# Second Fourier axis folded once more: five short matmuls in place of four long ones, joined on VectorE

**Chip, cores, metric.** One core of a Trainium2 chip. The metric is the device time of one execution in microseconds (us), median over several executions. In the lines of the profile PE is TensorE (the matmuls), DVE VectorE and ACT ScalarE (elementwise work), POOL GpSimd, and SPq the queue in which SyncE issues DMAs (copies); PSUM is the memory that the matmuls write.

## The reference, cut to what matters

Attention reads between `x` (8 batches, 512 rows, 8 heads of 64) and a small `state` (32 rows) give 544 rows of 512 for each batch. On these rows:

```python
X = np.fft.fft(x, axis=1)                 # first axis: the 544 rows
X = np.fft.fft(X, axis=2)                 # second axis: 512 columns
u = x + np.real(X)
un = (u - u.mean(-1)) / sqrt(u.var(-1) + 1e-6)
out = u + np.maximum(un @ w_ch1, 0.0) @ w_ch2     # 512 -> 2048 -> 512
```

## The kernel before: the parts concerned

Columns are folded once (d with 512-d), rows are folded too. `over_s` transforms along the rows, `over_d` along the columns (this is the "second axis"), `add` adds the input to it, `centre` takes statistics and writes the centred tile `ub` in bf16, and `turn_u` transposes it into `unT`, which the first MLP layer (`layer1`, PSUM tile `ph`) reads. `layer2` (PSUM tile `po`) ends in a store through `ot`.

```python
def fold():                                            # VectorE, once a batch
    nc.vector.tensor_add(Sm, XF, XR)
    nc.vector.tensor_add(XE[:, 0:2, :], Sm[:, :, 0:256], Sm[:, :, 512:256:-1])
    ...                                                # XO = difference, XN = middle column
def over_d(k):                                         # TensorE, twice a batch
    yp = yp_of[k] = qt("yp")
    for c in range(4):
        nc.tensor.matmul(yp, lhsT=G[:, c, 128 * k:128 * k + 128], rhs=T2[:, c, :],
                         start=(c == 0), stop=(c == 3))
def add(k, r):                                         # VectorE, PSUM + SBUF
    if r:
        nc.vector.tensor_add(U[k][:, 1, 1:512], yp[:, 1:512], XR[:, k, 1:512])
        nc.vector.tensor_add(U[k][:, 1, 512:513], yp[:, 0:1], XR[:, k, 512:513])
    else:
        nc.vector.tensor_add(U[k][:, 0, 0:512], yp, XF[:, k, 0:512])
...
for b in range(1, B + 1):       # a stage: layer 2 of batch b-1, layer 1 of b, reads and transform of b+1
    streams = [(layer2(b - 1) + ..., 0, 1)]
    streams.append((layer1(b), 0.08 if b == 1 else 0.02, 1))
    streams.append((reads_next, 0, 0.4))               # where in the stage a stream begins and ends
    streams.append((transform(b + 1), 0.45, 0.92))
    ...
    weave(*streams)             # sorts the steps of all streams: the order of issue
```

The softmax here doesn't subtract the row's maximum and nothing guards it: scores larger than these inputs give would overflow.

## Time and profile before

| | before |
|---|---|
| time, median of 3 runs | 329.02 us (328.88 to 329.29) |
| TensorE / VectorE / ScalarE busy | 96% / 51% / 44% |
| time of the profiled execution (its span) | 331.23 us (329.3 us) |
| first matmul of the second layer (`po`) begins | 61.8 us |
| from there to the end of the span | 267.5 us |

The table splits the span in two. Up to the first `po` the engines wait for each other; from it to the end TensorE has no visible gap, so a microsecond of TensorE work is a microsecond of time there. The lines themselves are in the prediction.

### The profile page before, as it was taken

Reading aid. Unit: us, or ns where it says so; the run is one execution under the profiler, and the core shown is the slowest. Engines: PE = TensorE matmul, PEld = TensorE weight load, DVE = VectorE, ACT = ScalarE, POOL = GpSimd, SP = SyncE. Lnnn points to the kernel's source line nnn. Section 1 sums busy time; section 2 is a strip of 40 time slices with the busy share of each in tenths; the row PEclk is TensorE's granted clock in tenths of the full one; section 3 lists DMA queues with packets and bytes.
Section 4 is the critical chain, followed back from the end, with each engine's and each line's share of the span. In section 5 each row is a group of like instructions: output and inputs, shape, how many; then the busy total and the mean of one; then the engine's idle time right before and its main releaser. Section 6 shows DMA issues by size and latency. Waiting matters only on the chain.

```text
span 329.3 us, 5692 instructions
## 1 busy us (share of the span) xinstructions
PE 315.1 (96%) x2204; PEld 182.2 (55%) x2204; DVE 169.0 (51%) x421; ACT 146.3 (44%) x279; POOL 62.8 (19%) x144
## 2 busy tenths in 40 slices
PE   6988969899999999999999999999999999999995
PEld 6776858645555554556555554545554544455444
DVE  8778575553755556671554728363855375100112
ACT  7897827844344344334344244434344423233300
POOL 3189732400240012200240003200210021000000
PEclk9999979999999999999999999999999999999999
DMA  7999999174155905259152433630241215222055
GB/s 150 171 145 216 159 196 187 32 157 100 48 104 120 180 2 113 50 130 169 50 112 66 97 66 79 128 82 32 64 98 36 60 50 112 58 57 64 34 118 137
DMA packets 107082, 33.15 MB, mean 101 GB/s; under 512 B 98480, under 2 KB 102832, under 8 KB 107056
## 3 DMA queue, kind: packets, MB, share of 16 engines
q1 hardware_dynamic: 96336, 27.03, 38.0%
q0 software_dynamic: 4224, 4.19, 8.0%
q10 hardware_dynamic: 6496, 1.57, 2.3%
q8 instruction: 17, 0.28, 0.4%
q14 instruction: 9, 0.07, 0.1%
HBM read 22.04 MB, written 13.63 MB: 108 GB/s over the span
## 4 chain that ended last, share of the span: by engine, by line
PE 84%; DVE 5%; DMA 4%; POOL 3%; SPq 2%; ACT 1%; issue 1%; DVEq 0%; POOLq 0%; ACTq 0%
PE po L646 35%; PE ph L580 32%; PE yp L473 3%; DMA xs<-in_x_dram 3%; PE gp L455 3%; PE ph L590 2%; PE eTp L331 2%; PE srp L378 2%; SPq L108 1%; PE xrp L359 1%; POOL w L269 1%; DMA out_dram<-ot 1%; PE xfp L359 1%; PE gp L459 1%; PE esp L342 1%
## 5 line engine op out<-in xcount | busy, mean ns | idle before, releaser
L646 PE MATMUL po<-w,hT 128*128 128x512 bf16 x496 | 125.2, 379 | 0.0
L582 ACT ACTIVATE hT<-ph 128x512 bf16<-128x512 f32 x112 | 66.8, 597 | 111.1 <-PE ph L580 111.0
L580 PE MATMUL ph<-unT,w 128*128 128x512 bf16 x448 | 115.0, 379 | 0.0
L580 PEld LDWEIGHTS <-w 128*128 128x128 bf16 x576 | 51.1, 98 | 50.0
L646 PEld LDWEIGHTS <-hT 128*128 128x128 bf16 x496 | 48.0, 98 | 45.5
L611 DVE SCALAR_TENSOR_TENSOR ot<-po,rstd,U 128x512 f32<-128x512 f32 (+1 forms) x33 | 24.2, 734 | 47.7 <-PE po L646 45.3
L465 POOL COPY GL<-G 128x128 bf16<-128x128 bf16 x8 | 2.4, 301 | 135.9 <-ACT G L463 135.9
L479 DVE TENSOR_TENSOR U<-yp,XR 128x511 f32<-128x511 f32 x16 | 10.9, 684 | 29.3 <-PE yp L473 29.3
L279 DVE BATCH_NORM_STATS2 st<-U 128x6 f32<-128x512 f32 x32 | 21.8, 682 | 0.1
L284 POOL TENSOR_TENSOR rstd<-rstd,mhalf 128x1 f32<-128x1 f32 x34 | 20.0, 588 | 2.7
L283 POOL TENSOR_TENSOR rstd<-mv,epst 128x1 f32<-128x1 f32 x34 | 7.2, 211 | 63.6 <-DVE mv L281 63.5
L590 PE MATMUL ph<-unT,w 128*128 128x128 bf16 x256 | 18.0, 228 | 0.0
L666 PE MATMUL warm<-ident 128*128 128x128 bf16 x172 | 14.2, 237 | 3.6 <-POOL ident masks.py:199 3.3
L463 ACT CAST G<-gp 128x288 bf16<-128x288 f32 x30 | 11.8, 398 | 12.0 <-PE gp L455 8.9
L590 PEld LDWEIGHTS <-w 128*128 128x128 bf16 x256 | 16.6, 103 | 0.5
L473 PE MATMUL yp<-T,G 128*128 128x512 bf16 x64 | 16.4, 379 | 0.0
L666 PEld LDWEIGHTS <-ident 128*128 128x128 bf16 x172 | 12.5, 108 | 4.9 <-POOL ident masks.py:199 3.3
L389 ACT ACTIVATE XR<-srp,rcs 32x64 bf16<-32x64 f32 x32 | 9.9, 309 | 10.3 <-DVE rcs L380 10.0
L359 PEld LDWEIGHTS <-ET 128*128 128x128 bf16 x80 | 7.3, 98 | 11.7 <-DVE XF L368 3.7
L117 POOL CAST xin<-xs 128x2048 bf16<-128x2048 f32 x7 | 13.2, 1890 | 0.0
L592 ACT ACTIVATE hT<-ph 128x512 bf16<-128x512 f32 x16 | 9.4, 604 | 8.0 <-PE ph L590 8.0
L492 DVE TENSOR_SCALAR ub<-U,mv 128x512 bf16<-128x512 f32 x24 | 12.3, 512 | 0.9
(137 smaller groups left out, 339.4 us busy)
## 6 DMA issues: line engine op xcount, KB each, us to landing
xs<-in_x_dram SPq DMA_DIRECT2D x30, 256.0 KB, 5.0
w<-in_moe_w_ch_dram POOLq DMA_DIRECT2D x8, 512.0 KB, 9.9
out_dram<-ot SPq DMA_DIRECT2D x15, 256.0 KB, 2.2
r_dram<-ot SPq DMA_DIRECT2D x14, 256.0 KB, 4.4
out_dram<-r_dram SPq DMA_DIRECT2D x14, 256.0 KB, 3.5
xs<-in_x_dram ACTq DMA_DIRECT2D x2, 256.0 KB
l_dram<-ot SPq DMA_DIRECT2D x2, 256.0 KB, 2.0
r_dram<-ot ACTq DMA_DIRECT2D x2, 256.0 KB
```

The costliest lines, as they stand in the source:

```text
L117: nc.gpsimd.tensor_copy(t[:, :, 1:513], xs)
L279: nc.vector.bn_stats(st6, u)
L284: nc.gpsimd.tensor_tensor(rstd, rstd, mhalf, op=ALU.pow)
L359: nc.tensor.matmul(ph[:, 0:260], lhsT=ET[:, g, c0:c0 + 128], rhs=rhs, start=True, stop=True)
L473: nc.tensor.matmul(yp, lhsT=G[:, c, 128 * k:128 * k + 128], rhs=T2[:, c, :], start=(c == 0), stop=(c == 3))
L492: nc.vector.tensor_scalar(t, in0=ud, scalar1=mv[:, 0:1], scalar2=None, op0=ALU.subtract)
L580: nc.tensor.matmul(ph[:, o:o + n], lhsT=w1[:, c, f * 128:(f + 1) * 128], rhs=un_of[key][:, c, :], start=(c == 0), stop=(c == DC - 1))
L582: nc.scalar.activation(hT[:, per * i:per * i + per, :].rearrange("p a b -> p (a b)"), ph, AF.Relu, scale=-1.0 if key in flipped else 1.0)
L590: nc.tensor.matmul(ph[:, o:o + 128], lhsT=w1[:, c, f * 128:(f + 1) * 128], rhs=un_of[key][:, c, 128 * r:128 * r + 128], start=(c == 0), st ...
L611: nc.vector.scalar_tensor_tensor(ot[:, cols], in0=po_of[i][:, 0:cols.stop - cols.start], scalar=rstd, in1=u[:, cols], op0=ALU.mult, op1=AL ...
L646: nc.tensor.matmul(po_of[i], lhsT=h_of[key][:, f, i * 128:(i + 1) * 128], rhs=w2[:, f, :], start=(f == 0), stop=(f == FC - 1))
L666: nc.tensor.matmul(t[:, 0:128], lhsT=ident, rhs=ident, start=(i == 0), stop=(i == n - 1))
```

## The change

The intent is less TensorE work. Even outputs of the second axis need only a cosine over d folded with 256-d, odd outputs the difference; so five matmuls of about 128 columns give all values, even ones in the first half of the PSUM bank and odd ones in the second. The price: the fold has a second step on VectorE (`XQ`), ScalarE copies the odd half to SBUF, and VectorE joins even and odd into `y` before the two additions. The order of issue is changed with it.

```diff
 def fold():
-    nc.vector.tensor_add(XE[:, 0:2, :], Sm[:, :, 0:256], Sm[:, :, 512:256:-1])
+    nc.vector.tensor_add(XE[:, 0:2, 0:256], Sm[:, :, 0:256], Sm[:, :, 512:256:-1])   # XE, XO now fp32
...
+    nc.vector.tensor_add(XQ[:, 0], XE[:, :, 0:128], XE[:, :, 256:128:-1])
+    nc.vector.tensor_sub(XQ[:, 1], XE[:, :, 0:128], XE[:, :, 256:128:-1])
...
+    nc.vector.tensor_sub(XQ[:, 2], XO[:, :, 0:128], XO[:, :, 256:128:-1])
+    nc.vector.tensor_add(XQ[:, 3], XO[:, :, 128:0:-1], XO[:, :, 128:256])
+def parts(g):
+    p = qt("yp")
+    nc.tensor.matmul(p[:, 0:129], lhsT=g[0], rhs=TE[:, 0:129], start=True, stop=False)
+    nc.tensor.matmul(p[:, 0:129], lhsT=g[2], rhs=TN, start=False, stop=True)
+    nc.tensor.matmul(p[:, 257:384], lhsT=g[2], rhs=TO[:, 0:127], start=True, stop=True)
+    nc.tensor.matmul(p[:, 129:257], lhsT=g[1], rhs=TE[:, 129:257], start=True, stop=True)
+    nc.tensor.matmul(p[:, 384:512], lhsT=g[3], rhs=TO[:, 127:255], start=True, stop=True)
+    odd = wk.tile([128, 256], F32, name="odd", tag="odd", bufs=1)
+    nc.scalar.copy(odd, p[:, 256:512])
+def whole(p, odd):
+    y = wk.tile([128, 514], F32, name="y", tag="y", bufs=1)
+    nc.vector.tensor_add(y[:, 0:256] as (n r), even, odd)          # written shorter here
+    nc.vector.tensor_sub(y[:, 512:256:-1] as (n r), even, odd)
+    ...                                                            # two tiny copies
 def add(k, r):
-        nc.vector.tensor_add(U[k][:, 1, 1:512], yp[:, 1:512], XR[:, k, 1:512])
+        y_of[k] = whole(*yp_of[k])
+        nc.vector.tensor_add(U[k][:, 1, 1:513], y_of[k][:, 1:513], XR[:, k, 1:513])
...                                                # sines of the tables moved, low fold of batch 1 put later
-          (reads_next, 0.2, 0.55), (transform(1), 0.58, 1.0)
+          (reads_next, 0.2, 0.52), (transform(1), 0.54, 0.92)
-            streams.append((reads_next, 0, 0.4)); streams.append((transform(b + 1), 0.45, 0.92))
+            streams.append((reads_next, 0, 0.37)); streams.append((transform(b + 1), 0.41, 0.81))
```

More of the change, by code (lines that the diff above doesn't have):

```diff
@@ L66 @@
     mhalfpi = singles.tile([128, 1], F32, name="mhalfpi")
-    pi_ = singles.tile([128, 4], I32, name="pi_")
+    pi_ = singles.tile([128, 5], I32, name="pi_")
     gen1 = wk.tile([128, 4096], F32, name="gen1", tag="hT")
@@ L70 @@
     lt = gen1[:, 3072:3072 + NM].bitcast(I32)
-    li = gen2[:, 3072:3072 + dm].bitcast(I32)
+    li = gen2[:, 3072:3072 + 385].bitcast(I32)
     nc.gpsimd.iota(lt[:, 0:256], pattern=[[1, 256]], base=1, channel_multiplier=0)
@@ L75 @@
     nc.gpsimd.iota(pi_[:, 3:4], pattern=[[0, 1]], base=0, channel_multiplier=1)
+    nc.gpsimd.iota(pi_[:, 4:5], pattern=[[0, 1]], base=128, channel_multiplier=-1)
     for hh in range(4):
         nc.gpsimd.iota(pi_[32 * hh:32 * hh + 32, 2:3], pattern=[[0, 1]], base=256, channel_multiplier=1)
-    nc.gpsimd.iota(li, pattern=[[1, dm]], base=0, channel_multiplier=0)
+    nc.gpsimd.iota(li[:, 0:129], pattern=[[2, 129]], base=0, channel_multiplier=0)
+    nc.gpsimd.iota(li[:, 129:257], pattern=[[2, 128]], base=1, channel_multiplier=0)
+    nc.gpsimd.iota(li[:, 257:385], pattern=[[2, 128]], base=1, channel_multiplier=0)
     make_identity(nc, ident)
@@ L83 @@
     nc.gpsimd.memset(mhalf, -0.5)
-    stf = singles.tile([128, B, 2, D], F32, name="stf")
+    stf = gen2[:, 1024:2048].rearrange("p (b g d) -> p b g d", b=B, g=2)
     def load_state(lo, hi):
@@ L163 @@
     XFs, XRs, XLs = two("XF", [128, 2, 514]), two("XR", [128, 2, 514]), two("XL", [128, 514])
-    XEs, XOs, XNs = two("XE", [128, 3, 256]), two("XO", [128, 3, 256]), two("XN", [128, 3, 128])
+    XE, XO = singles.tile([128, 3, 257], F32, name="XE"), singles.tile([128, 3, 257], F32, name="XO")
+    XQs, XNs = two("XQ", [128, 4, 3, 128]), two("XN", [128, 3, 128])
     GLs = [singles.tile([128, 4, 128], BF16, name=f"GL{i}") for i in range(2)]
@@ L169 @@
     ST = singles.tile([128, 2, NM], BF16, name="ST")
-    T2 = singles.tile([128, 4, dm], BF16, name="T2")
-    pf = singles.tile([128, 4], F32, name="pf")
+    TE = singles.tile([128, 257], BF16, name="TE")
+    TO = singles.tile([128, 255], BF16, name="TO")
+    TN = singles.tile([128, 129], BF16, name="TN")
+    pf = singles.tile([128, 5], F32, name="pf")
     cl1 = gen1[:, 2048:2048 + NM // 2].bitcast(BF16)
@@ L197 @@
     f1, q1 = turn(NM, Stot, lt, [0, 1, 2], gen1)
-    f2 = gen2[:, 0:dm]
-    q2_ = gen2[:, dm:2 * dm]
-    nc.vector.tensor_scalar(f2, in0=li, scalar1=pf[:, 3:4], scalar2=None, op0=ALU.mult)
+    f2 = gen2[:, 0:385]
+    q2_ = gen2[:, 512:897]
+    nc.vector.tensor_scalar(f2[:, 0:257], in0=li[:, 0:257], scalar1=pf[:, 3:4], scalar2=None, op0=ALU.mult)
+    nc.vector.tensor_scalar(f2[:, 257:385], in0=li[:, 257:385], scalar1=pf[:, 4:5], scalar2=None, op0=ALU.mult)
     nc.vector.tensor_scalar(q2_, in0=f2, scalar1=1.0 / dm, scalar2=float(1 << 23), op0=ALU.mult, op1=ALU.add)
@@ L222, in more_sines @@
         w = 2.0 * PI / dm * shrink
-        nc.scalar.activation(T2[:, 0, :], q2_, AF.Sin, bias=halfpi, scale=-w)
-        nc.scalar.activation(T2[:, 2, :], f2, AF.Sin, bias=0.0, scale=-w)
-        c4 = [T2[:, i, :].rearrange("p (n r) -> p r n", r=4) for i in range(4)]
-        for r in range(4):
-            near, far = (0, 2) if r % 2 == 0 else (2, 0)
-            nc.scalar.activation(c4[1][:, r, :], c4[near][:, r, :], AF.Copy, scale=1.0 if r < 2 else -1.0)
-            nc.scalar.activation(c4[3][:, r, :], c4[far][:, r, :], AF.Copy, scale=1.0 if r in (0, 3) else -1.0)
+        nc.scalar.activation(TE, q2_[:, 0:257], AF.Sin, bias=halfpi, scale=-w)
+        nc.scalar.activation(TO[:, 0:127], f2[:, 1:128], AF.Sin, bias=0.0, scale=-w)
+        nc.scalar.activation(TO[:, 127:255], f2[:, 257:385], AF.Sin, bias=0.0, scale=-w)
         nc.scalar.activation(gate2[:, 3:4], gate2[:, 0:1], AF.Exp)
     def alternate():
-        alt = T2[0:1, 2, :].rearrange("p (n two) -> p two n", two=2)
-        nc.gpsimd.memset(alt[:, 0, :], 1.0)
-        nc.gpsimd.memset(alt[:, 1, :], -1.0)
+        nc.gpsimd.memset(TO[0:1, 127:255:2], -0.5)
+        nc.gpsimd.memset(TO[0:1, 128:255:2], 0.5)
     nc.gpsimd.tensor_copy(gate, q2_[:, 0:4])
@@ L243, in clears @@
         nc.gpsimd.memset(XLs[i][:, 512:514], 0.0)
-        nc.gpsimd.memset(XEs[i][:, 2, :], 0.0)
-        nc.gpsimd.memset(XOs[i][:, 2, :], 0.0)
-        nc.gpsimd.memset(XOs[i][:, 0:2, 0:1], 0.0)
+        if i == 0:
+            nc.gpsimd.memset(XE[:, 2, :], 0.0)
+            nc.gpsimd.memset(XO[:, 2, :], 0.0)
+            nc.gpsimd.memset(XO[:, 0:2, 0:257:256], 0.0)
+            nc.gpsimd.memset(TN, 0.0)
+            nc.gpsimd.memset(TN[0:1, 0:129:2], 1.0)
+            nc.gpsimd.memset(TN[0:1, 1:129:2], -1.0)
         nc.gpsimd.memset(XNs[i].rearrange("p a b -> p (a b)"), 0.0)
@@ L256, in more_loads @@
     def more_loads():
-        nc.gpsimd.tensor_copy(gate[:, 0:1], XNs[0][:, 0, 0:1])
+        nc.gpsimd.tensor_copy(gate[:, 0:1], XQs[0][:, 3, 0, 0:1])
         alternate()
@@ L297, in attend @@
         XF, XR, XL = XFs[b % 2], XRs[b % 2], XLs[g4]
-        XE, XO, XN = XEs[b % 2], XOs[b % 2], XNs[b % 2]
+        XQ, XN = XQs[b % 2], XNs[b % 2]
         sb = stb[:, b, :, :]
@@ L303, in attend @@
         E = wk.tile([128, 4, 2, 128], BF16, name="E", tag="E")
-        Sm = wk.tile([128, 2, 514], BF16, name="Sm", tag="Sm")
+        Sm = wk.tile([128, 2, 514], BF16, name="Sm", tag="Sm", bufs=1)
         def turn_state():
@@ L385, in sread @@
                     i = p[ph, 1 - g + 64 * hh:65 - g + 64 * hh]
-                    if g == 0:
+                    if g == 0 and b > 0:
                         nc.vector.tensor_scalar(o, in0=i, scalar1=rcs[ph, g:g + 1], scalar2=None, op0=ALU.mult)
@@ L392, in low @@
             xread(256 - 32 * bq, False, "xlp", XL[pq, 0:512], pq)
-            if b:
+            if b > 1:
                 fold_low(True)
@@ L398, in fold_low @@
             if even:
-                nc.vector.tensor_add(XE[pq, 2, :], XL[pq, 0:256], XL[pq, 512:256:-1])
+                nc.vector.tensor_add(XE[pq, 2, 0:256], XL[pq, 0:256], XL[pq, 512:256:-1])
+                nc.vector.tensor_copy(XE[pq, 2, 256:257], XL[pq, 256:257])
             else:
                 nc.vector.tensor_sub(XO[pq, 2, 1:256], XL[pq, 1:256], XL[pq, 511:256:-1])
-                nc.vector.tensor_copy(XN[pq, 2, 0:1], XL[pq, 256:257])
         def fold():
             nc.vector.tensor_add(Sm, XF, XR)
-            nc.vector.tensor_add(XE[:, 0:2, :], Sm[:, :, 0:256], Sm[:, :, 512:256:-1])
-            if b == 0:
+            nc.vector.tensor_add(XE[:, 0:2, 0:256], Sm[:, :, 0:256], Sm[:, :, 512:256:-1])
+            nc.vector.tensor_copy(XE[:, 0:2, 256:257], Sm[:, :, 256:257])
+            if b < 2:
                 fold_low(True)
+            nc.vector.tensor_add(XQ[:, 0], XE[:, :, 0:128], XE[:, :, 256:128:-1])
+            nc.vector.tensor_sub(XQ[:, 1], XE[:, :, 0:128], XE[:, :, 256:128:-1])
+            nc.vector.tensor_copy(XN[:, :, 0:1], XE[:, :, 128:129])
+            if b < 2:
                 fold_low(False)
             nc.vector.tensor_sub(XO[:, 0:2, 1:256], Sm[:, :, 1:256], Sm[:, :, 511:256:-1])
-            nc.vector.tensor_copy(XN[:, 0:2, 0:1], Sm[:, :, 256:257])
+            nc.vector.tensor_sub(XQ[:, 2], XO[:, :, 0:128], XO[:, :, 256:128:-1])
+            nc.vector.tensor_add(XQ[:, 3], XO[:, :, 128:0:-1], XO[:, :, 128:256])
         first = ([] if b >= x_by_dma else [turn_state, lambda: turn_x(0), lambda: turn_x(1)]) + [
@@ L431, in attend @@
         return first, second
+    def parts(g):
[7 more added lines that the diff above has]
+        nc.scalar.copy(odd, p[:, 256:512])
+        return p, odd
+    def whole(p, odd):
+        y = wk.tile([128, 514], F32, name="y", tag="y", bufs=1)
+        even = p[:, 0:258].rearrange("p (r n) -> p r n", n=129)[:, :, 0:128]
+        odd = odd.rearrange("p (r n) -> p r n", n=128)
+        nc.vector.tensor_add(y[:, 0:256].rearrange("p (n r) -> p r n", r=2), even, odd)
+        nc.vector.tensor_sub(y[:, 512:256:-1].rearrange("p (n r) -> p r n", r=2), even, odd)
+        nc.vector.tensor_copy(y[:, 0:257:256], p[:, 0:129:128])
+        nc.vector.tensor_copy(y[:, 512:513], p[:, 0:1])
+        return y
     un_of, tiles_of = {}, {}
@@ L440, in transform @@
         XF, XR = XFs[b % 2], XRs[b % 2]
-        XE, XO, XN = XEs[b % 2], XOs[b % 2], XNs[b % 2]
+        XQ, XN = XQs[b % 2], XNs[b % 2]
         G = wk.tile([128, 4, NM], BF16, name="G", tag="G")
@@ L451, in over_s @@
             p = qt("gp")
-            X, tab = (XE, cos) if j < 2 else (XO, sin)
-            jj = j % 2
+            tab = cos if j < 2 else sin
             for c in range(3):
-                nc.tensor.matmul(p[:, 0:NM], lhsT=X[:, c, 128 * jj:128 * jj + 128], rhs=tab[c],
+                nc.tensor.matmul(p[:, 0:NM], lhsT=XQ[:, j, c, :], rhs=tab[c],
                                  start=(c == 0), stop=(c == 2 and j != 2))
@@ L465, in over_s @@
                 nc.gpsimd.tensor_copy(GLs[g4][:, :, 32 * bq:32 * bq + 32], G[:, :, 256:NM])
-        yp_of = {}
+        yp_of, y_of = {}, {}
         def over_d(k):
             U[k] = wk.tile([128, 2, 514], F32, name="U", tag="U", bufs=5)
-            yp = yp_of[k] = qt("yp")
-            for c in range(4):
-                nc.tensor.matmul(yp, lhsT=G[:, c, 128 * k:128 * k + 128], rhs=T2[:, c, :],
-                                 start=(c == 0), stop=(c == 3))
+            yp_of[k] = parts([G[:, c, 128 * k:128 * k + 128] for c in range(4)])
         def add(k, r):
-            yp = yp_of[k]
             if r:
-                nc.vector.tensor_add(U[k][:, 1, 1:512], yp[:, 1:512], XR[:, k, 1:512])
-                nc.vector.tensor_add(U[k][:, 1, 512:513], yp[:, 0:1], XR[:, k, 512:513])
+                y_of[k] = whole(*yp_of[k])
+                nc.vector.tensor_add(U[k][:, 1, 1:513], y_of[k][:, 1:513], XR[:, k, 1:513])
             else:
-                nc.vector.tensor_add(U[k][:, 0, 0:512], yp, XF[:, k, 0:512])
+                nc.vector.tensor_add(U[k][:, 0, 0:512], y_of[k][:, 0:512], XF[:, k, 0:512])
         def centre(k, r):
@@ L546, in over_d @@
         def over_d():
-            yp = qt("yp")
-            for c in range(4):
-                nc.tensor.matmul(yp, lhsT=GLs[g4][:, c, :], rhs=T2[:, c, :], start=(c == 0), stop=(c == 3))
+            yp = parts([GLs[g4][:, c, :] for c in range(4)])
             U = m["U"] = wk.tile([128, 512], F32, name="UL", tag="UL", bufs=1)
-            nc.vector.tensor_add(U, yp, XLs[g4][:, 0:512])
+            nc.vector.tensor_add(U, whole(*yp)[:, 0:512], XLs[g4][:, 0:512])
         def centre():
@@ L675 @@
     weave((warmed(s0[:4], 8) + s0[4:], 0, 1), ([lambda: state_blocks(1, 2, nc.vector.tensor_copy)], 0.6, 0.6))
-    weave((warmed(r0, 4), 0, 1), ([sines], 0.01, 0.01), ([more_sines], 0.3, 0.3), ([lambda: warm(56)], 1, 1))
+    weave((warmed(r0, 4), 0, 1), ([sines], 0.25, 0.25), ([more_sines], 0.3, 0.3), ([lambda: warm(56)], 1, 1))
     more_loads()
@@ L681 @@
     scores_next, reads_after = attend(2)
-    weave((layer1(0), 0, 1), (t0[10:], 0.02, 0.25), (s1[3:], 0.0, 0.16), (reads_next, 0.2, 0.55),
-          (transform(1), 0.58, 1.0), ([lambda: cast_x(2)], 0.1, 0.1), (scores_next, 0.55, 0.97),
+    weave((layer1(0), 0, 1), (t0[10:], 0.02, 0.25), (s1[3:], 0.0, 0.16), (reads_next, 0.2, 0.52),
+          (transform(1), 0.54, 0.92), ([lambda: cast_x(2)], 0.1, 0.1), (scores_next, 0.55, 0.97),
           ([lambda: state_ones(2, B)], 0.5, 0.5), ([lambda: load_x(4)], 0.8, 0.8))
@@ L690 @@
         if b + 1 < B:
-            streams.append((reads_next, 0, 0.4))
-            streams.append((transform(b + 1), 0.45, 0.92))
+            streams.append((reads_next, 0, 0.37))
+            streams.append((transform(b + 1), 0.41, 0.81))
         if b + 2 < B:
```

## The prediction

> **What bounds the kernel now.** I read the busy shares first, then the slices, then the waits from 60 us on, then the timelines of 20 to 62 us, because a saved TensorE microsecond counts only where TensorE is what everything waits for.
>
> ```profile
> PE 315.1 (96%) x2204; PEld 182.2 (55%) x2204; DVE 169.0 (51%) x421; ACT 146.3 (44%) x279; POOL 62.8 (19%) x144
> PE   6988969899999999999999999999999999999995
> DVE  8778575553755556671554728363855375100112
> PEclk9999979999999999999999999999999999999999
> ```
>
> TensorE is busy 96% of the span; VectorE and ScalarE about half. A busy TensorE need not be at its peak, so I check the pitch: in the chain in order of time, four 512-column matmuls take 0.86 us, and sixteen of 128 columns 0.89 us. With those pitches (216 ns and 56 ns) the matmuls after the first of the second MLP layer, at 61.8 us, sum to 263.8 us, and the span ends 267.5 us after it. From there on TensorE does nothing but stream. The waits of 60 to 310 us agree: the other engines wait for TensorE, and what TensorE waits for is under 2 us in all.
>
> ```profile
> ACT hT L582 <- PE ph L580: 109.9, 104, 2.3
> DVE ot L611 <- PE po L646: 42.0, 17, 7.1
> DVE U L479 <- PE yp L473: 23.7, 7, 6.2
> PE tp L501 <- ACT E L347: 0.7, 1, 0.7
> ```
>
> The first 60 us are another regime: 1-in-10 idle slices, dummy matmuls [...], and one dip of the clock (the 7 in the last line above). [...]
>
> ```profile
> 41.01 1.90 POOL L117 CAST xin<-xs 128x2048 bf16<-128x2048 f32 x1
> 41.09 1.96 DVE L399 TENSOR_TENSOR XE<-XL 32x256 bf16<-32x256 bf16 x1
> 44.34 0.60 PE L359 MATMUL xrp<-stb,ET 128*128 128x260 bf16 x2 [2.90 <-DVE XF L368]
> 44.73 1.91 PE L590 MATMUL ph<-unT,w 128*128 128x128 bf16 x16
> 53.79 0.69 DVE L479 TENSOR_TENSOR U<-yp,XR 128x511 f32<-128x511 f32 x1 [3.51 <-PE yp L473]
> ```
>
> A small fold of batch 1, 0.28 us elsewhere, takes 1.96 us beside a GpSimd cast; TensorE stands 2.90 us behind it and then runs sixteen matmuls in 1.7 us instead of 0.89. From 53.8 to 59.7 VectorE is busy without a gap and the transposes of batch 1 wait for it.
>
> [...] Trace: 512 bf16 elements 441 ns, 512 fp32 677 to 690 ns, 1028 bf16 696 ns. [...]
>
> **The change, part by part.**
>
> *TensorE, second axis.* Eighteen groups (16 tiles, 2 of low rows) lose 4 x 216 = 863 ns and gain 5 x 56 = 280 ns. Sum removed: 72 x 0.2157 = 15.5 us; added: 90 x 0.056 = 5.0 us; net 10.5 us. The groups of batches 0 and 1 (four, 2.3 us) lie before 61.8 us, where TensorE waits for others anyway. The other fourteen save 14 x 0.583 = 8.2 us in the saturated stretch. Counted over the instruction order of the changed kernel with the same pitches, the work from the first matmul of the second layer on is 255.6 us against 263.8: 8.2 again.
>
> *VectorE.* Folding: XE and XO are now fp32, so those ops drop from 0.44 and 0.42 to about 0.69 us; four joins into XQ of 384 fp32 elements, [...]; small copies and the low rows about 0.45. Together about 3.2 us a batch. Joining even and odd: two ops of 256 fp32, about 424 ns each (the trace has 424 for 128x256), two tiny copies of about 0.15, less the 146 ns tail add: about 1.0 us for a tile. A batch gains 3.2 + 2 x 1.0 = 5.2 us; the sum with the low rows is about 43 us, VectorE going from 169 to about 210 us, two thirds of the span. In a steady batch of 34 us it is 24.5 instead of 19.3: still not the bound on average.
>
> *ScalarE.* A copy of 256 columns out of PSUM for each group, about 0.38 us (288 columns take 398 ns): 7 us. Eight table copies of 0.53 us go. About even.
>
> *Steady stage, does TensorE wait?* In the instruction order, from the end of a fold's last read to the first matmul on XQ there are 3.4 us of TensorE work in most batches; VectorE needs 0.15 + 0.25 + 0.69 + 0.72 (Sm) + 0.72 (XE) + 0.1 + 0.57 = 3.2 us. Tight, but it fits, save batch 2, where only 2.4 us stand there: about 0.9 us lost. The last centred tile plus the 2.4 us landing of its transposing DMA ends 0.5 to 1 us ahead of the first matmul that needs it. I allow 1.2 us for the whole stretch.
>
> *Start, batch 0.* Four XR copies of 0.29 us leave VectorE's chain for ScalarE, so Sm starts at about 19.3 instead of 20.0 us. The fold then takes about 4.6 us instead of 1.4 and ends near 24.5 (22.1 before); the G copies on VectorE follow. The matmuls of the second axis end near 26.1 instead of 25.1; the odd copy and the join add 0.45 + 1.05, so the first addition moves from 25.1 to about 27.7. The second tile, behind the first on both VectorE and ScalarE (whose order puts the odd copy behind a centring), comes about 3.4 us later than before. TensorE: about +3.2 us at 35 us.
>
> *Start, batch 1.* The low fold leaves the spot where the cast blocked it, which returns most of the 2.90 us: reads that ended at 44.6 end near 45 to 46. But now 3.9 us of VectorE work lie between that read and the first matmul on XQ, and the order has one group of sixteen (0.89 us) to fill it: a new wait of about 3 us; that matmul, at 48.2 before, comes at 48.5 to 50. Then the join: VectorE was full for 5.95 us there, and gets 0.5 us more lead and about 1.9 us more work, so the last transpose, 7.6 us behind the second-axis matmul before, is about 9.2 behind it. The first matmul of the second layer comes at 64 to 67 instead of 61.8 us: +2.2 to +5.2.
>
> *Sum.* 329.0 - 8.2 + 1.2 + (2.2 to 5.2) = 324.2 to 327.2 us. Working by hand through in-order queues, I have probably made the start too stiff, and the new weave fractions look like those of someone who tuned on the chip; I move a little down and say 324.5.
>
> **The rivals.**
>
> *A: the full gain arrives.* If the start comes out even, because the freed 2.9 us and the unthrottled clock (about 1.5 us) pay for the longer fold, the time is 329.0 - 8.2 = 320.8 us, down to 319 if batch 1 gains too. For it: TensorE is saturated in 80% of the span, and the changes in the start (ScalarE takes copies, sines moved, the low fold put later) aim at just this. Against it: VectorE bounds much of 14 to 26 and 54 to 60 us, and all of its additions are serial there.
>
> *B: VectorE becomes the bound in each batch.* A 5.5 us burst (read, fold, joins) ahead of the store that frees a PSUM bank, one y and one odd buffer, and ScalarE in order behind an odd copy that waits for VectorE. With 1 us lost in each of six batches it would be 329 to 331 us. For it: the margins of 0.2 to 1 us. Against it: VectorE has idle gaps of 2 to 4 us in every batch (207.8, 215.2, 227.1, 230.8 us in the timeline), and transform was moved earlier to use them.
>
> *C: contention with GpSimd.* [...] From 25 to 35 us GpSimd is nearly always busy; four additions could lose 0.4 us each. That gives 326 to 328.
>
> **Range and chances.** The saturated gain of 8.2 is firm to half a microsecond; the start is loose by 3 either way, the steady waits by 1 to 3. So 80%: 319.5 to 328.5 us. Two per cent is 322.4 us: reached only if the start costs less than about 0.5 us with no steady waits, or somewhat more if batch 1 gains. I give that 0.32; slower by 2% would need rival B at its worst, 0.03.
>
> **What would show it right or wrong.** Right: the second-axis group in 0.28 us; VectorE near 210 us; the first matmul of the second layer at 64 us or later; from there to the end about 259 to 260 us; TensorE waiting some 3 us for XQ in batch 1 and about 1 us for it in batch 2; no 1.96 us fold. Rival A: that matmul at or before 62 us. Rival B: repeated waits of TensorE for VectorE or ScalarE after 65 us, 1 us or more in each batch. Rival C: additions or joins over 1 us beside GpSimd instructions. The prediction fails if the pitch of the short matmuls is far above 56 ns, or if the joins cost well off 424 ns.

## The result

| | before | after |
|---|---|---|
| time, median of 4 runs | 328.95 us (328.69 to 329.29) | 347.67 us (345.76 to 349.14) |
| span of the profiled run | 329.3 us | 345.5 us |
| first `po` begins | 61.8 us | 71.4 us |
| from there to the end | 267.5 us | 274.1 us |

The changed kernel is slower: ratio 1.0565, 95% interval 1.0512 to 1.0618. (Here and below a ratio is the mean time of one kernel's runs over the mean of the other's of the same rounds, so it is not quite the ratio of the medians quoted.)

The page of the changed kernel, busy time and slices of 8.6 us:

```profile
PE 310.6 (90%) x2192; PEld 181.4 (52%) x2222; DVE 205.7 (60%) x514; ACT 149.2 (43%) x294; POOL 62.8 (18%) x147
PE   5975958699998999999999999999979998999996
DVE  8797677438593669576573669556945867300021
PEclk9998999699999999999999999999999999999999
```

TensorE has less to do, though not by 10 us: its busy time includes slow-clock stretches (and 30 of its 2222 matmuls left no record). It is busy for 90% of a longer span; digits of 7 and 8 stand where there were only nines. VectorE went from 169.0 to 205.7 us. There is a new dip of the clock (6) at the end of the start. By the trace TensorE ran at half its clock from 32.6 to 36.0 and from 63.3 to 70.1 us, 10.2 us in all, which can have cost at most half of that, 5.1 us (an estimate).

The parts themselves cost what they were meant to. TensorE's timeline (start, duration, line, output and inputs) shows the first and the last of the five matmuls of a tile and what follows:

```profile
91.92 0.22 PE L450 MATMUL yp<-TE,G 128*128 128x129 bf16 x1
92.15 0.22 PE L454 MATMUL yp<-TO,G 128*128 128x128 bf16 x1
92.21 1.02 PE L675 MATMUL po<-w,hT 128*128 128x512 bf16 x4
```

From 91.92 to 92.21 are 0.29 us for the five (0.86 before for the four). VectorE's timeline for the same tile:

```profile
93.02 0.42 DVE L463 TENSOR_TENSOR y<-yp,odd 128x256 f32<-128x256 f32 x1 [1.33 <-ACT odd L456]
93.36 0.42 DVE L464 TENSOR_TENSOR y<-yp,odd 128x256 f32<-128x256 f32 x1
94.00 0.69 DVE L511 TENSOR_TENSOR U<-y,XR 128x512 f32<-128x512 f32 x1
94.61 0.68 DVE L513 TENSOR_TENSOR U<-y,XF 128x512 f32<-128x512 f32 x1
```

The joins take 0.42 us each; with the two tiny copies the first addition begins 0.98 us after the join did. And VectorE starts only when ScalarE's odd copy is there, at 93.0, 0.8 us after the five matmuls gave way to the next (92.21).

What is new are TensorE's waits. The waits from 66 us on (engine, line, releaser: us in total, times, longest); in the kernel before TensorE's matmuls had no such entry at all; two waits for `tp`, 1.2 us before the first `po`, are left out:

```profile
PE ph L609 <- DMA unT<-ub: 6.5, 5, 2.2
PE xrp L366 <- DVE XF L375: 2.4, 5, 0.6
PE ph L609 <- DVE ot L640: 1.1, 2, 0.8
PE gp L490 <- DVE XQ L418: 0.6, 1, 0.6
PE xfp L366 <- DVE XL L375: 0.5, 3, 0.2
```

The first layer waits for transposed tiles (`unT`). Adding every gap over 0.12 us in TensorE's timeline after the first `po` gives 11.5 us in 18 gaps, and zero in the kernel before. The saving of 8.2 us should have left 259.3 us there; 274.1 are 14.8 more. The gaps account for nearly all of it: a gap is counted from the modelled end of a matmul, 0.38 us after its start at 512 columns, although the next one could have started after 0.22. Counted from start to start, less the pitch, the same 18 gaps are 14.4 us.

**How `unT` comes late.** In the steady batch above, the second axis begins at 91.92 and the last of the four tiles is centred at 103.88, 11.96 us later; before it was 10.47 us (82.89 to 93.36).

```profile
101.71 0.74 DVE L640 SCALAR_TENSOR_TENSOR ot<-po,rstd,U 128x512 f32<-128x512 f32 x1
103.37 0.51 DVE L523 TENSOR_SCALAR ub<-U,mv 128x512 bf16<-128x512 f32 x1
108.61 1.02 PE L609 MATMUL ph<-unT,w 128*128 128x512 bf16 x3 [1.44 <-DMA unT<-ub]
```

The kernel before:

```profile
82.89 1.03 PE L473 MATMUL yp<-T,G 128*128 128x512 bf16 x4
92.85 0.51 DVE L492 TENSOR_SCALAR ub<-U,mv 128x512 bf16<-128x512 f32 x1
```

Then the transposing DMAs: the SyncE queue of the changed kernel (start, duration of the issue)

```profile
96.82 1.24 SPq L528 DMA_TRANSPOSE unT<-ub  x1
102.48 0.35 SPq L655 DMA_DIRECT2D r_dram<-ot  x1
102.88 4.18 SPq L528 DMA_TRANSPOSE unT<-ub  x3
```

and of the kernel before, in the same batch:

```profile
87.82 0.34 SPq L626 DMA_DIRECT2D r_dram<-ot  x1
88.25 7.22 SPq L497 DMA_TRANSPOSE unT<-ub  x4
```

In the changed kernel a store of a result (`ot`) stands ahead of three transposes and waits for VectorE, which makes `ot` only at 101.71. The second tile was centred at 98.2, yet its transpose waits until 102.88; and three transposes then take 4.18 us to issue, about 1.4 each. With the 2.4 us from issue to landing the first layer goes on at 108.61, 4.73 us after the last tile was centred. In the kernel before the store was in front of all four: it held the first for 1.5 us (centred at 86.75, issued at 88.25), and TensorE waited for none.

**The start.** TensorE's timeline in batch 1 (in brackets: idle before, and its releaser):

```profile
60.98 0.40 PE L532 MATMUL tp<-ident,ub 128*128 128x128 bf16 x4 [1.45 <-ACT ub L521]
63.30 0.58 PE L532 MATMUL tp<-ident,ub 128*128 128x128 bf16 x4 [1.25 <-ACT unT L533]
63.69 1.91 PE L619 MATMUL ph<-unT,w 128*128 128x128 bf16 x16
68.27 1.91 PE L619 MATMUL ph<-unT,w 128*128 128x128 bf16 x16
```

After gaps of 1.45 and 1.25 us the clock drops: sixteen short matmuls take 1.91 us, where the same line at full clock shows 1.06. The first gap ends with the centring of the first tile, which comes late after join, additions and statistics on VectorE. To the later ones a loop between two engines adds, for ScalarE keeps the order of the program in this trace: the last of the second tile's five matmuls starts at 58.41 and takes 0.22 us, ScalarE stands idle for 1.64 us up to 60.20, and yet that tile's odd copy comes only at 61.92. ScalarE's timeline:

```profile
60.20 0.72 ACT L521 ACTIVATE ub<-U,mv 128x512 bf16<-128x512 f32 x1 [1.64 <-DVE mv L288]
61.30 0.71 ACT L521 ACTIVATE ub<-U,mv 128x512 bf16<-128x512 f32 x1
61.92 0.36 ACT L456 COPY odd<-yp 128x256 f32<-128x256 f32 x1
```

The odd copy of the second tile sits in ScalarE's queue behind two centrings (and an `ET` activation, not shown), which wait for VectorE's statistics of the first tile (`mv`); VectorE's join of the second tile waits for that copy (1.35 us of idle at 62.31). Each engine stands while the other works. How little this loop is worth by itself is seen below (a_oddearly, a_joinonly).

### The profile page after: what moved, and what is told of

It reads as the page before. It is cut to its first block, busy times and chain, and to the rows that moved or that the text cites. A ratio compares the mean times of both kernels' runs of the same rounds, so it can differ in the third digit from the quotient of the medians.

```text
span 345.5 us, 5807 instructions
## 1 busy us (share of the span) xinstructions
PE 310.6 (90%) x2192; PEld 181.4 (52%) x2222; DVE 205.7 (60%) x514; ACT 149.2 (43%) x294; POOL 62.8 (18%) x147
## 5 line engine op out<-in xcount | busy, mean ns | idle before, releaser
L675 PE MATMUL po<-w,hT 128*128 128x512 bf16 x482 | 123.6, 379 | 0.8
L611 ACT ACTIVATE hT<-ph 128x512 bf16<-128x512 f32 x112 | 66.8, 597 | 123.4 <-PE ph L609 121.7
L619 PE MATMUL ph<-unT,w 128*128 128x128 bf16 x256 | 19.4, 237 | 0.0
L695 PE MATMUL warm<-ident 128*128 128x128 bf16 x172 | 15.0, 245 | 3.7 <-POOL ident masks.py:199 3.5
L498 ACT CAST G<-gp 128x288 bf16<-128x288 f32 x30 | 11.5, 398 | 13.7 <-PE gp L490 9.1
L396 ACT ACTIVATE XR<-srp,rcs 32x64 bf16<-32x64 f32 x36 | 11.1, 309 | 13.0 <-DVE rcs L387 12.6
L463 DVE TENSOR_TENSOR y<-yp,odd 128x256 f32<-128x256 f32 x18 | 7.5, 419 | 13.8 <-ACT odd L456 13.8
L490 PEld LDWEIGHTS <-XQ 128*128 128x128 bf16 x96 | 8.3, 98 | 12.4 <-DVE XQ L418 6.2
L366 PEld LDWEIGHTS <-ET 128*128 128x128 bf16 x80 | 6.5, 98 | 15.5 <-DVE XF L375 6.7
L318 DVE COPY sT<-sTp 128x512 bf16<-128x512 bf16 x7 | 3.0, 424 | 16.1 <-PE sTp L317 16.0
```

The source lines that it names most:

```text
L490: nc.tensor.matmul(p[:, 0:NM], lhsT=XQ[:, j, c, :], rhs=tab[c], start=(c == 0), stop=(c == 2 and j != 2))
L498: nc.scalar.copy(G[:, j, :], p[:, 0:NM])
L611: nc.scalar.activation(hT[:, per * i:per * i + per, :].rearrange("p a b -> p (a b)"), ph, AF.Relu, scale=-1.0 if key in flipped else 1.0)
L619: nc.tensor.matmul(ph[:, o:o + 128], lhsT=w1[:, c, f * 128:(f + 1) * 128], rhs=un_of[key][:, c, 128 * r:128 * r + 128], start=(c == 0), st ...
L675: nc.tensor.matmul(po_of[i], lhsT=h_of[key][:, f, i * 128:(i + 1) * 128], rhs=w2[:, f, :], start=(f == 0), stop=(f == FC - 1))
L695: nc.tensor.matmul(t[:, 0:128], lhsT=ident, rhs=ident, start=(i == 0), stop=(i == n - 1))
```

## The experiments

Unless said otherwise a number in brackets is the median of the kernel before in the same rounds. "Wrong result" means wrong on purpose. `po` and the rest of the span are from each profiled run.

| run | what it is | time, us | ratio (95%) | first `po` | rest of span |
|---|---|---|---|---|---|
| b_short | before, short matmuls only (wrong result) | 320.22 (329.01) | 0.976 (0.971 to 0.981) | 58.8 | 259.4 |
| a_nojoin_ow | changed, no join, old order (wrong result) | 328.32 (329.07) | 0.997 (0.995 to 1.000) | 64.5 | 262.7 |
| a_nojoin | changed, no join (wrong result) | 333.64 (329.01) | 1.014 (1.013 to 1.016) | 66.2 | 265.8 |
| b_weave | before, new order | 337.52 (329.25) | 1.025 (1.021 to 1.029) | 63.4 | 271.6 |
| a_oddonly | changed, ScalarE's half of the join (wrong result) | 337.11 (328.94) | 1.021 (1.015 to 1.028) | 66.9 | 266.3 |
| a_joinonly | changed, VectorE's half of the join (wrong result) | 342.26 (328.94) | 1.036 (1.029 to 1.043) | 71.2 | 271.4 |
| a_oldweave | changed, old order | 346.56 (329.07) | 1.053 (1.048 to 1.058) | 70.9 | 274.2 |
| v_halves2 | own version, right | 326.25 (329.07) | 0.992 (0.989 to 0.995) | 62.1 | 263.0 |

### 1. Is TensorE's saving real? b_short

```diff
-            for c in range(4):
-                nc.tensor.matmul(yp, lhsT=G[:, c, ...], rhs=T2[:, c, :], ...)
+            short(yp, [G[:, c, ...] for c in range(4)])   # the five short matmuls, on the old tables
```

> The kernel before with nothing changed but the second axis: its four 512-column matmuls become five of about 128 columns into the same bank (result wrong on purpose; folds, additions and order as before). If the TensorE saving is real where nothing else is added: 329.0 - 8.2 (14 groups in the saturated stretch at 0.583 us) to 329.0 - 10.5, that is 318.5 to 321 us. Rival, the short matmuls cost more than their 56 ns (weights reloaded, bank handling): 324 us or more.

Measured 320.22 us: 8.8 us less. From the first `po` to the end 259.4 us in place of 267.5: 8.1 us, the 8.2 of the prediction. The saving is real, and it is lost elsewhere.

### 2. The join left out, in the new and in the old order: a_nojoin, a_nojoin_ow, a_oldweave, b_weave

```diff
# a_nojoin
-        odd = wk.tile(...); nc.scalar.copy(odd, p[:, 256:512]); return p, odd
+        return p, None
# and whole(p, odd) returns p: the additions read PSUM as before
# a_oldweave: the changed kernel with the old places in the stage; b_weave: the reverse on the kernel before
-            streams.append((reads_next, 0, 0.37)); streams.append((transform(b + 1), 0.41, 0.81))
+            streams.append((reads_next, 0, 0.4)); streams.append((transform(b + 1), 0.45, 0.92))
```

> The changed kernel without the join: no odd copy on ScalarE, no y; the additions read the PSUM bank as before (result wrong on purpose). Folding stays. If the join's chain (ScalarE copy, then 1.05 us on VectorE for each tile) is what delays the start and the transposes: the start gains about 3 to 4 us, the waits for unT (7 us) mostly go, so 334 to 339 us. Rival, the longer fold does most of the harm: 343 us or more.

> The kernel before with only the order of the changed kernel (its weave fractions for reads and transform, its place of the sines), right result. If the new order costs in itself (reads closer to each other, xrp then waits behind the low fold; read and first second-fold matmul closer): 331 to 334 us. Rival, the order is harmless and only the added work counts: 328.5 to 330 us.

> The changed kernel with the order of the kernel before (weave fractions and place of the sines). The order alone cost the kernel before about 8 us. Theory 1, the order is costly in itself (reads and second axis closer together, VectorE and TensorE waiting for each other): 338 to 342 us here too, and waits for XF at the reads fall from 0.56 to about 0.2 us. Theory 2, the change needs its earlier order, since the join lengthens the way from the second axis to the first layer: the waits of the first layer for transposed tiles grow from about 6.5 to over 10 us in all, and the time is 347 us or more.

> The changed kernel without odd copy and join (wrong result on purpose) and with the order of the kernel before: what is left of the change is the long fold of VectorE and the short matmuls. If the order is the costly part and the fold is not, 324 to 327 us against 333.6 with the new order (the new order alone cost 8 us on the kernel before). If the fold needs the new order, the waits for XQ show at every batch (0.5 to 1.5 us) and it stays at 330 to 334 us.

The run a_nojoin (333.64 us) came out just under its 334 to 339; a_nojoin_ow (328.32) lies between its two theories. The four runs, with b_short and the two kernels, take the loss apart. In the old order: short matmuls alone -8.8 us; the fold with its second step +8.0 (a_nojoin_ow, 0.75 us under its kernel before, less b_short); the join +18.2 (a_oldweave less a_nojoin_ow). Together +17.5. The new order on top, 346.56 to 347.67, is within the intervals: no difference shown.

In the new order the join costs 14.0 us (347.67 - 333.64). So the new order does help the join by about 4 us, and costs about 5 without it (333.64 against 328.32) and 8.3 on the kernel before. The expectation for b_weave, 331 to 334, was too low. Its timeline shows where a part goes, in waits from 66 us on that the kernel before lacks:

```profile
PE xrp L359 <- DVE XF L368: 1.6, 5, 0.5
PE xfp L359 <- DVE XL L368: 0.7, 4, 0.2
```

The reads, squeezed into 0.37 of the stage, wait for VectorE's previous read. These 2.3 us are gaps from the modelled end of a matmul; counted from start to start, less the pitch, they are 4.0 us, nearly all of the 4.1 us by which the rest of the span grew (271.6 against 267.5). For a_oldweave both theories stated failed as put: the time stayed (so the order is not what costs in the changed kernel), and TensorE's gaps after the first `po` were 10.6 us in place of 11.5, under partly other names.

### 3. Which half of the join? a_oddonly, a_joinonly

```diff
# a_oddonly: a_nojoin with the odd copy put back
+        odd = wk.tile(...); nc.scalar.copy(odd, p[:, 256:512])
# a_joinonly: the changed kernel, the join reads a constant tile
-        odd = wk.tile(...); nc.scalar.copy(odd, p[:, 256:512]); return p, odd
+        return p, odd0
```

> The changed kernel with the odd copy of ScalarE kept and VectorE's join left out: the additions read the PSUM bank as in the run without a join (wrong result on purpose). Nobody waits for the copy but the next copy in its buffer. If the copy costs by the time it takes from ScalarE (18 x 0.38 us, nearly all beside other work), it is 333.6 to 335 us, as without copy and join. A rival: the copy holds up ScalarE's centrings and copies of the start; then it is over 337 us.

> The changed kernel with VectorE's join kept and the odd copy of ScalarE left out: the join reads a constant tile in its place (wrong result on purpose). It tells the two halves of the join's 14 us apart. If VectorE's longer serial work is what costs, most of it stays: 342 to 346 us, the first matmul of the second layer at 69 us or later and waits of the first layer for transposed tiles as in the changed kernel. If the hop to ScalarE is what costs (VectorE waits 1.4 to 1.8 us for the odd copy several times in the start), it falls to 335 to 339 us, and that matmul comes at 67 us or earlier.

Over a_nojoin, ScalarE's half adds 3.5 us and VectorE's 8.6; the two add up to 12.1 of 14.0. VectorE's serial work is the main half: a_joinonly has its first `po` at 71.2 us, as late as the changed kernel, without any hop to ScalarE for odd values. (Its profiled execution is the slowest of its four, 345.14 us, with 13.7 us at half clock before that point, 10.2 in the changed kernel; so 71.2 is an upper end.) The hop is a smaller part and not nothing; my expectation of at most 335 us without VectorE's half missed, and the rival stated with it, over 337 us, came. The clock is not what tells these runs apart: executions with a mean granted clock of 0.988 to 0.990 took 333.1 to 334.3 us in a_nojoin, 336.66 and 337.56 in a_oddonly, 342.13 and 342.39 in a_joinonly. The profiled execution of a_oddonly shows little of the 3.5 us: it was a quick one, with a span only 1.2 us above that of a_nojoin, and TensorE's waits for ScalarE in batch 1 were 1.25, 0.78 and 0.71 us against 0.34 and 0.71 there.

### 4. The store ahead of the transposes: a_latestore

```diff
-                queue.dma_start(out=r_dram[b, k], in_=ot)
-                later.append(...)                      # copy back to the output
+                later.append(put)                      # the store itself is issued one store later
```

> The changed kernel, right result; each output store is issued one store later, so that the DMA queue of SyncE never waits for VectorE's store in front of a transposing DMA. If the transposes are late because they stand behind a store that waits for VectorE (three of them then issue one after the other, 1.2 us each): most of the 7.3 us that TensorE loses for unT goes, 340 to 342.5 us. Rival, the centred tiles themselves are late on VectorE: 345.5 us or more.

Measured 345.27 us (329.01), ratio 1.051 (1.048 to 1.054): 2.4 us less than the changed kernel, not the 5 to 8 expected, and the two intervals overlap (1.051 to 1.062 there), so that even this gain is not clear of noise. The result is right. The waits say why the gain is small (the same view as above, this run):

```profile
PE ph L609 <- DVE ot L642: 3.7, 3, 2.6
PE ph L609 <- DMA unT<-ub: 0.2, 1, 0.2
```

The waits for `unT` went from 6.5 to 0.2 us, as meant; a wait for `ot` rose from 1.1 to 3.7 us. The PSUM bank that `ph` wants is freed by VectorE's `ot`, and VectorE is in its burst of joins and statistics at that time. So the queue order is where the loss appears and not what makes it: read from these waits, the same long stretch of VectorE stands behind both.

### 5. Smaller suspects: a_lowlate, a_oddearly, a_bf16

```diff
# a_lowlate: the low rows always folded inside fold(), not after their read
-            if b > 1: fold_low(True); fold_low(False)
# a_oddearly: in batches 0 and 1 the second tile's matmuls and odd copy come before the first tile's join
-            lambda: (over_d(0), add(0, 1), add(0, 0)),
+            lambda: (over_d(0), over_d(1) if b == 1 else None, add(0, 1), add(0, 0)),
# a_bf16: XE and XO in bf16
-    XE, XO = singles.tile([128, 3, 257], F32), singles.tile([128, 3, 257], F32)
+    XE, XO = singles.tile([128, 3, 258], BF16), singles.tile([128, 3, 258], BF16)
```

> The changed kernel, right result; the low rows are folded inside the fold for every batch and no more between two reads. If the 0.9 us that they stand in front of the next read's eviction cause the waits of TensorE for xrp and xfp (about 4 us in five batches): 343 to 345 us, with the wait for XQ up by at most 0.5 us a batch. Rival, the time is only moved to XQ: 347 to 348.5 us.

> The changed kernel, right result; for batches 0 and 1 alone the second tile's matmuls and its odd copy are issued right after the first tile's, so that ScalarE does not hold the odd copy behind centrings that wait for VectorE. If that queue order is a good part of the join's harm in the start (VectorE waited 0.96 and 1.35 us for odd there, TensorE 1 to 2 us after it): first matmul of the second layer at 68 to 70 instead of 71.4 us, total 344.5 to 346 us. Rival, the serial work on VectorE alone decides: 347 us or more.

> The changed kernel with XE and XO in bf16 instead of fp32, [...] a fold takes about 3.2 instead of 4.6 us. Right result if the tolerance allows the extra rounding. If the length of the fold is what TensorE waits for in the start and at XQ: 1.3 us in each of batches 0 and 1, 1 us in the batches: 341 to 344.5 us. Rival, the fold's harm is in the order, not in its length: 346 us or more.

a_lowlate: 349.5 us (329.01), ratio 1.062; two executions took 347.3 us (clock 0.985) and two 351.7 (0.976). The waits for `XF` fell from 2.4 to 0.8 us and waits for `XQ` rose from 0.6 to 2.2: moved, not removed. a_oddearly: 347.02 us (329.25), ratio 1.053; the first `po` came 1.1 us earlier (70.3), the total within the spread. TensorE's gaps in batch 1 stayed, 1.40, 1.52 and 0.71 us, and so they did in a_joinonly, which has no odd copy at all (1.00, 1.52, 0.71): the loop of the two engines is a small part of the late start. a_bf16: 346.56 us (329.25), ratio 1.049 (1.042 to 1.055); the fold's additions into `XQ` fell from 552 to 564 ns each to 353 to 367, those into `XE` and `XO` from 695 and 683 to 429 and 419, the largest wait for `XQ` in batch 1 only from 2.83 to 2.24 us. None of the three is the cause by itself. All three are right.

### 6. A version without the join: v_halves, v_halves2, v_halves3

The join exists because even and odd outputs are sums that PSUM could make. With only the input side folded once more, two 256-column matmuls accumulate the even outputs and two the odd ones; no odd copy, no `y`, and XE and XO in bf16. v_halves writes even and odd outputs to every second PSUM column:

```diff
+    def halves(yp, g):
+        for r in range(2):
+            for c in (r, r + 2):
+                nc.tensor.matmul(yp[:, r:512:2], lhsT=g[c], rhs=T2[:, c, :], start=(c == r), stop=(c == r + 2))
```

> A version of my own, right result: the kernel before with the second fold (into XQ, in bf16 throughout) but without any join. Four matmuls of 256 columns a tile (even outputs from the two parts with even columns, odd outputs from the two others, written to every second column of the bank) replace four of 512. If the join does the harm and the fold can be borne: the groups cost 4 x 109 = 436 ns instead of 863, 14 x 0.427 = 6.0 us less in the saturated stretch, the fold costs about 1.6 us on VectorE in batches 0 and 1: 322 to 326 us. Rival, any second fold costs as much as in a_nojoin (13 us over b_short): 333 us or more.

A miss: 333.87 us (329.25), ratio 1.013 (1.009 to 1.016). TensorE's timeline of it, the group of four and the next one:

```profile
197.12 1.03 PE L448 MATMUL yp<-T,G 128*128 128x256 bf16 x4
197.94 0.64 PE L332 MATMUL eTp<-xT,sT 128*128 128x288 bf16 x4
```

0.82 us for four matmuls of 256 columns, 205 ns each, hardly less than one of 512 (216). v_halves2 writes contiguous columns and lets VectorE's additions interleave:

```diff
-                nc.tensor.matmul(yp[:, r:512:2], ...)
+                nc.tensor.matmul(yp[:, 256 * r:256 * r + 256], ...)
-                nc.vector.tensor_add(U[k][:, 0, 0:512], yp, XF[:, k, 0:512])
+                nc.vector.tensor_add(mixed(U[k][:, 0, 0:512]), apart_(yp), mixed(XF[:, k, 0:512]))
# mixed: "p (n r) -> p r n", apart_: "p (r n) -> p r n", both with r=2
```

> The own version with the four 256-column matmuls of a group written to contiguous PSUM columns (even outputs in the first 256, odd in the second), and the four additions of a tile reading and writing through a permuted view instead. If the stride of the PSUM output was what kept the group at 0.82 us, the group now takes about 0.44 us and the fourteen groups of the saturated stretch save 14 x 0.38 = 5.3 us on the 333.9 us of the strided version: about 328.5 us, near the kernel before. The additions must stay near 0.68 us [...]. Rival: 256-column matmuls with a reloaded weight are slow by themselves; then the group stays at 0.8 us and the time at 333 to 334 us. A second rival: the permuted views slow the additions to over 1 us; then waits for U and unT appear and the time is 331 or more.

```profile
193.09 0.60 PE L448 MATMUL yp<-T,G 128*128 128x256 bf16 x4
193.52 0.60 PE L332 MATMUL eTp<-xT,sT 128*128 128x288 bf16 x4
```

Now 0.43 us, 108 ns each (109 expected for v_halves). VectorE's interleaving additions stay at 677 to 686 ns. 326.25 us (329.07), better than the 328.5 expected, the right result and faster than both kernels: by 0.8% against the one before, and about 6% against the changed one, which ran in other rounds. The visible gaps after the first `po` are 0.7 us in all.

v_halves3 tried to win the start as well: the GpSimd cast that stretches a small fold of batch 1 issued earlier.

```diff
         nc.gpsimd.tensor_copy(gate, xs_of[2][:, :, 0])
+        cast_x(2)                                       # before the loads of the second weights
-            streams.append((transform(b + 1), 0.45, 0.92))
+            streams.append((transform(b + 1), 0.46, 0.92))
```

> The own version with contiguous halves (326.2 us, right), and two changes of order: GpSimd's cast of the third batch's x is issued before the loads of the second weights instead of beside the small fold of batch 1 (1.95 us there instead of 0.28, and TensorE waits 2.82 us behind it), and the second axis of each later batch begins a little later (0.46 instead of 0.45 of the stage), which should take away the four waits of 0.18 us. If the wait of 2.82 us goes without a new one, 323.5 to 325 us; if the wait for XQ behind it (1.01 us) grows to 2 us instead, 325 to 326.

A miss: 326.74 us (328.94), ratio 0.991 (0.985 to 0.996), the same as v_halves2. The fold fell from 1.95 to 0.29 us and the wait behind it from 2.82 to 1.16 us, yet the read that precedes it (`srp` of batch 1) came 1.74 us later, and the first `po` stayed at 62.2. The clock made that read late: in this execution TensorE ran at half clock from 29.5 to 32.9 us, which can cost up to 1.7 us (an estimate, half of that stretch), and never in the profiled one of v_halves2; it was 0.23 us behind before that stretch (26.91 against 26.68). Still, the executions at a mean clock of 1.000 show no gain either: 325.78 and 325.99 us against 325.26 and 325.52 of v_halves2. Where the freed wait went in them has no trace.

## Why the prediction was wrong, point by point

- **TensorE's saving: right.** 8.2 us predicted for the saturated stretch, 8.1 in b_short; the group in 0.29 us.
- **VectorE's costs: right.** "VectorE going from 169 to about 210 us": 205.7. Joins 0.42 us against 424 ns; the additions into `XQ`, of 384 fp32 elements, 552 to 564 ns, between the 424 ns of 256 elements and the 677 to 690 of 512 in the kernel before.
- **"I allow 1.2 us for the whole stretch": the step that failed most.** 14.8 us were lost there, 14.4 of them in the 18 gaps. I compared single margins ("ends 0.5 to 1 us ahead of the first matmul that needs it"), each against the chain as it stood alone. The 2.4 us landing was taken from the last centred tile; in the trace 4.73 us lie between, because these transposes need 1.2 to 1.4 us each to issue and a store that waits for VectorE stands among them in the queue (the second tile, centred at 98.2, had its transpose issued at 102.88, after the store at 102.48). a_latestore shows that this queue is only where the loss appears: without it 2.6 us more fell to the next consumer of VectorE's work.
- **Start, batch 1: right in kind, too small.** The wait for `XQ` was 2.83 us ("about 3 us"). But "the last transpose, 7.6 us behind the second-axis matmul before, is about 9.2 behind it": it was 11.3, beside gaps of TensorE that end with VectorE's and ScalarE's work and with sixteen matmuls at half clock, and the first `po` came at 71.4, not 64 to 67. How much of this each of them cost was not measured; breaking the loop (a_oddearly) brought 1.1 us. The prediction also measured the start from 61.8, which a half-clock stretch had made about 2 us late.
- **Weave fractions: wrong.** "Look like those of someone who tuned on the chip": I moved the number down for it. b_weave shows that the order costs 8.3 us by itself; in the changed kernel it gains nothing that shows.
- **Rival B** ("VectorE becomes the bound in each batch") was the one that came, at over twice its size in the steady part (14.8 us against 6 in six batches); the start, which it left out, lost more than half as much again. I argued against it with VectorE's average share and its gaps of 2 to 4 us. Those gaps lie outside the burst: VectorE is idle while waiting for the second axis and full from there to the last centred tile, and only that stretch counts. a_joinonly is the run that shows it: VectorE's half of the join costs 8.6 us at 60% busy. **Rival A** is excluded by the first `po`. **Rival C** was small: one addition of 1.21 us beside a cast, a mean of 724 ns over all sixteen against 684 before.
- **In sum**, the predicted -4.5 became +18.7: in the profiled runs the start is 9.6 us later (2.2 to 5.2 predicted; nearer 12 against a usual execution of the kernel before), the rest 6.6 longer in place of 7.0 shorter.

What stays open: how the start's loss divides between the longer fold, the join and the half clock, and why the two halves of the join fall 1.9 us short of the whole (the intervals of these runs are about 2 us wide each way; by the ratios the halves are 2.4 and 7.3 us, and two executions of the kernel before took 331.6 and 331.8 us in those rounds).

## What to carry to other kernels

Work taken from a saturated engine and put on one that is half idle is free only if it doesn't lengthen the stretch from that engine's input to the next thing the saturated engine needs; read that stretch, from producer to consumer with every queue in it, not the busy share. Let PSUM accumulate what an elementwise join would have to add (326.25 us here, 347.67 with the join), and keep the matmul's output contiguous (108 ns at 256 columns here, 205 with a step of two), leaving an interleave to an fp32 addition that is there anyway (677 to 686 ns here with it, 677 to 684 without). When a removed wait comes back under another name, look for the engine that stands behind both.

## What the traces show of pitch, clock and queue

- The pitch of matmuls with contiguous outputs was 56 ns at 128 columns, 108 at 256 and 216 at 512. With a PSUM output in steps of two columns (v_halves) it was 205 ns at 256 columns.
- The length of a gap alone does not settle whether TensorE's clock is halved, and no run here shows what does. The clock was halved at a gap of 2.90 us (kernel before: the gap ends at 44.34, the half clock begins at 44.39) and of 2.83 us (a_joinonly), and stayed full after 2.83 us (changed kernel) and 2.82 us (v_halves2). In the start of the changed kernel it was halved after gaps of 1.45 and 1.25 us; in a_joinonly it stayed full at 1.00, 1.52 and 0.71. The stretches at half clock in the profiles of the two kernels lasted 3.41 us (before) and 3.41 and 6.83 us (changed). In a_oldweave, whose TensorE timeline follows, it was halved after 3.13 us: the twelve matmuls of 512 columns from 293.06 us on take 4.28 us in place of 2.59 (twelve at 216 ns), so another 1.7 us is lost behind the gap.

```profile
292.20 1.02 PE L609 MATMUL ph<-unT,w 128*128 128x512 bf16 x4 [3.13 <-DVE mv L288]
293.06 1.55 PE L675 MATMUL po<-w,hT 128*128 128x512 bf16 x4
294.41 1.91 PE L609 MATMUL ph<-unT,w 128*128 128x512 bf16 x4
296.11 1.39 PE L675 MATMUL po<-w,hT 128*128 128x512 bf16 x4
297.34 1.03 PE L609 MATMUL ph<-unT,w 128*128 128x512 bf16 x4
```

- One transposing DMA of a 128x512 bf16 tile from SBUF to SBUF holds the SyncE queue for 1.23 us: the median of the changed kernel's 24 such issues from 66 us on (1.19 to 2.62; 4.18 for the three above). So a burst of them costs more than the landing time of the last, 2.4 us.
